# A 2-D spectral filter and a bilinear GLU on one core: down products gathered at five places of a chunk pair, and layer-norm operations one at each place

## The chip, the core and the metric

The kernel runs on one core of a Trainium2 chip. The metric is device time in microseconds for one execution. The kernel before takes 677.42 us, the median of three runs (677.13 to 677.56).

## The reference, cut to what matters

```
def _A_ref(x, w_r, w_i):
    X = rfft2(x) ; X = X * (w_r + 1j * w_i)
    return irfft2(X, s=(S, D))
def _B_ref(x, w_gate, w_up, w_down):
    g = x @ w_gate ; u = x @ w_up
    return (g * u) @ w_down
x = A_x                                   # S = 2048 tokens, D = 640, F = 1728
h  = x + _A_ref(_layernorm(x), A_w_r, A_w_i)
h2 = h + _B_ref(_layernorm(h), B_w_gate, B_w_up, B_w_down)
```

Everything is float32. The kernel splits each matmul operand into a high and a low part and multiplies high by high, high by low and low by high, so one product of 128 rows is three matmuls.

## The kernel before

Stages one and two (to about 190 us) are the spectral filter. Stage three is the bilinear GLU and takes the rest. Its 2048 tokens are two blocks of 1024, and its hidden width of 1728 is cut into chunks of 128; twelve whole chunks are taken as six pairs (`p` = 0 to 5), and a chunk pair is one step. The last columns are a step of their own (`p` = 6), which comes first in each block. Nothing reorders the work: every engine executes its instructions in the order in which this program writes them, and waits on counters of the other engines.

**Gate and up products.** `strassen()` (L1069) computes gate and up of one chunk with seven products on TensorE, six or nine matmuls of 512 columns each. Their sums live in PSUM banks from `single()`, four of them in rotation, of which a chunk takes three: `oa`, `ob` and `oc`. In traces these matmuls write `e`. ScalarE copies and VectorE additions and multiplications take the sums out: the copies `h0` (L1099), `c22` (L1109) and `h1` (L1116), and the VectorE lines L1119, L1122, L1123, L1129 and L1144. L1144 is the last reading of `oa`; it multiplies what the seventh product left there. In an odd chunk VectorE works out the seven left operands of the down products as well (L1131, L1134, L1155, and L1063 for the low parts, into the tile `ht`).

**Places.** After product n of a chunk the program calls `at(n)` (L1073), n from 1 to 7. Down products of the step before, layer-norm operations and preparations of weights (`side`) are hung there. So `at(1)` of a chunk stands between its first and its second product, and `at(7)` between its last product and the first of the next chunk.

**Down products.** A step's hidden activations meet the down weights one step later, beside the next pair's gate and up products. `down_products()` (L1025) does this with the seven-product algorithm, for two quarters of the tokens (`a` and `b`) in one call: fourteen products of three matmuls of 320 columns each. A step with such a pair before it (ten of the fourteen steps: `p` = 1 to 5 in both blocks) makes two calls, so 28 products. Each writes a PSUM bank from `lane()`, four banks, in traces `d`; a VectorE addition (L1044) then takes the whole bank into the residual rows `x`. A call uses a bank again and again, first clearing it or accumulating on what is there, so each product but the first in a bank waits for the addition before it in that bank. The order within a call is p1a p5a p1b p5b p6a p3a p6b p3b p7a p2a p7b p2b p4a p4b; p1, p6, p7 and p4 share one bank for `a` and one for `b`, p5, p3 and p2 the others. L1050 cuts a call into five pieces of 3, 3, 3, 2 and 3 products. L1303 and L1304 hang the ten pieces of a step at places 1 to 7 of the even chunk and 2 to 4 of the odd one.

**Layer norm of the second block.** While block 0 runs, the 32 small operations for the layer norm of block 1 (mostly `bn_stats` and `bn_aggr` on VectorE, L176 to L180) wait in a queue `fill`, and `at()` pops them from there. What is left is popped ahead of chunk 6.

Of the kernel before, what the change touches and what calls it, by code (L numbers as in the profile page):

```python
# [78 lines left out]
def tile_spectral_glu(ctx: ExitStack, tc: tile.TileContext, x, wre, wim, wgu, wlast, wdown, wdlast,  # L79
# [26 lines left out]
    def single():  # L106
        return bank("e", 4)
# [4 lines left out]
    def wk(shape, name):  # L112
        return work.tile(shape, F32, tag="wk", name=name)
# [4 lines left out]
    def mmx(o, l, r, start, stop):  # L118
        nc.tensor.matmul(o, l, r, start=start, stop=stop, skip_group_check=True)  # L119
# [3 lines left out]
    def pop(n=1):  # L123
        for _ in range(n):
            if fill:
                fill.popleft()()
# [87 lines left out]
    def front(ts, k):  # L214
        n = len(ts)
        r = small.tile([P, n], F32, tag="r", name="r")
        junk = [fold[:, o:o + D] for o in (NR * 1026, NR * 1026 + D)]
        m2, ve, fs = moments(ts, junk * 2 if k < n else None, k=k)
        for i, t in enumerate(ts):
            SC[t] = r[:, i:i + 1], m2[:, i:i + 1]  # L220
        return fs, inverse_root(ve, r, n)
# [10 lines left out]
    def even(t):  # L232
        f, j = folded(t)
        fs = [(0.47, lambda: nc.vector.scalar_tensor_tensor(view(f, 0, [[321, 2], [1, 161]]),
                                                     view(XP[t], 0, [[320, 2], [1, 161]]), SC[t][1],
                                                     view(XP[t], 640, [[-320, 2], [-1, 161]]),
                                                     op0=OP.subtract, op1=OP.add))]
        fs.append((0.14, lambda: tt(j[:, 0:64], f[:, 128:192], f[:, 449:513], op=OP.add)))
        fs.append((0.4, lambda: tt(view(j, 64, [[1, 2], [2, 160]]), view(f, 161, [[-161, 2], [1, 160]]),
                                   view(f, 482, [[-161, 2], [1, 160]]), op=OP.subtract)))  # L240
        return fs
# [58 lines left out]
    for ts, when, aside, root in GROUPS:  # L300
        k = len(when)
        fs, cs = front(ts, k)
# [15 lines left out]
    for t in range(NT):  # L318
        if t == 1:
            nc.gpsimd.dma_start(frall, frem)  # L320
        if t >= 1:
            fs = even(t)
# [422 lines left out]
    def scale_shift(ts, junk, total=None):  # L745
        n = len(ts)
        r = small.tile([P, n], F32, tag="r", name="r")
        b = small.tile([P, n], F32, tag="b", name="b")
        m2, ve, fs = moments(ts, junk, total)
        cs = inverse_root(ve, r, n)  # L750
        cs.append(lambda: nc.vector.scalar_tensor_tensor(b, m2, -0.5, r, op0=OP.mult, op1=OP.mult))
        for i, t in enumerate(ts):
            SC[t] = r[:, i:i + 1], b[:, i:i + 1]
        return fs, cs
# [108 lines left out]
    for ts in (range(3), range(3, 6), range(6, 8)):  # L863
        n, t0 = len(ts), ts[-1] + 1
        fs, cs = scale_shift(ts, [scrap] * n, total[:, ts[0]:t0])
# [120 lines left out]
    def operand(sb, k):  # L986
        return xt[:, sb, k, 0], xt[:, sb, k, 1]
# [71 lines left out]
    def hi_of(src, a):  # L1059
        act(hop[:, a, 0], src, AF.Copy)  # L1060

    def lo_of(src, a, engine=nc.vector):
        engine.tensor_tensor(hop[:, a, 1], src, f32(hop[:, a, 0]), op=OP.subtract)  # L1063
# [5 lines left out]
    def strassen(c, blk, ahead, downs, side):  # L1069
        wa, ws = W[c]  # L1070
        p, odd = divmod(c, 2)

        def at(n):  # L1073
            if downs.get(n):
                for f in downs[n]:
                    f()
                if c:
                    pop(2 if c in (2, 4) else 1)
            for f in side.get(n, ()):
                f()  # L1080

        b11, b21, b22 = ([operand(sb, k + i) for i in range(2)] for sb, k in ((0, 0), (0, 2), (1, 2)))
        t1, t2 = ([(TJ["12"][:, 0, m, k], TJ["12"][:, 1, m, k]) for k in range(2)] for m in range(2))
        t4 = [operand(1, k) for k in range(2)]
        b5 = [operand(sb, 4) for sb in range(2)]

        def product(o, first, w, a, ms, extra=()):
            terms = [(w, a + P * i, m) for i, m in enumerate(ms)] + list(extra)
            n = len(terms)
            for i, (w, a, m) in enumerate(terms):  # L1090
                whi, wlo = w[:, 0, a:a + P], w[:, 1, a:a + P]
                mmx(o, whi, m[0], first and i == 0, False)
                mmx(o, whi, m[1], False, False)
                mmx(o, wlo, m[0], False, i == n - 1)

        oa = single()
        product(oa, True, wa, 384, b11)
        h0 = wk([P, 512], "h0")
        act(h0, oa, AF.Copy)  # L1099
        for f in side.get(0, ()):  # L1100
            f()
        if ahead and c:
            ahead[0]()
            ahead[1]()
        at(1)
        ob = single()
        product(ob, True, ws, 256, t1, [(wa, 896, b5[1])])
        c22 = wk([P, 512], "c22")
        act(c22, ob, AF.Copy)  # L1109
        if not c:  # L1110
            ahead[0]()
            ahead[1]()
        at(2)
        product(oa, False, ws, 0, t2)
        h1 = wk([P, 512], "h1")
        act(h1, oa, AF.Copy)  # L1116
        at(3)
        product(ob, False, ws, 896, b22, [(ws, 512, b5[1])])
        tt(ob, ob, h1, op=OP.add)  # L1119
        at(4)  # L1120
        product(oa, False, ws, 640, [(t3[k][:, 0], t3[k][:, 1]) for k in range(2)])
        tt(c22, oa, c22, op=OP.add)  # L1122
        tt(ob if odd else h1, ob, c22, op=OP.mult)  # L1123
        if odd:
            hi_of(ob, 2 if p < 5 else 4)
        at(5)
        oc = single()
        product(oc, True, wa, 0, b21, [(wa, 256, b5[0])])
        tt(h0, oc, h0, op=OP.add)  # L1129
        if odd and p < 5:  # L1130
            tt(oc, ob, HELD["a21"], op=OP.add)  # L1131
            hi_of(oc, 3)
            lo_of(ob, 2)
            tt(ob, ob, HELD["s3"], op=OP.subtract)  # L1134
            hi_of(ob, 4)
            lo_of(oc, 3)
        elif odd:
            lo_of(ob, 4)
        if ahead and not odd:
            ahead[2]()  # L1140
            ahead[3]()
        at(6)
        product(oa, False, wa, 640, t4, [(wa, 896, b5[0])])
        tt(oa if c == 11 else h0, oa, h0, op=OP.mult)  # L1144
        if not odd:
            HELD["a11"], HELD["a21"] = h0, h1
            if p < 5:
                nc.gpsimd.tensor_tensor(c22, h0, h1, op=OP.subtract)
                HELD["s3"] = c22
        at(7)  # L1150
        if odd and p < 5:
            hi_of(h0, 1)
            lo_of(ob, 4)
            act(oc, h0, AF.Copy)
            tt(ob, h0, ob, op=OP.subtract)  # L1155
            hi_of(ob, 6)
            lo_of(oc, 1)
            lo_of(ob, 6)
        elif odd:
            hi_of(oa, 5)  # L1160
            lo_of(oa, 5)
# [5 lines left out]
    for n, (blk, p) in enumerate(steps):  # L1167
        if p == 6:
# [121 lines left out]
            if blk == 0:  # L1290
                fs, cs = scale_shift(range(8, 16), None)
# [5 lines left out]
        slots = [{}, {}]  # L1297
        if prev[1] == 6:
            fs = [[lambda j=j, prev=prev: down(*prev, j)] for j in range(8)]
            slots = [dict(zip(range(4, 8), fs[0:3] + [fs[3] + fs[4]])), dict(zip((2, 3, 4), fs[5:]))]  # L1300
        else:
            fs = down_products(*prev, (0, 1)) + down_products(*prev, (2, 3))
            slots[0] = dict(zip(range(1, 8), fs))  # L1303
            slots[1] = dict(zip((2, 3, 4), fs[7:]))  # L1304
        for ci in range(2):
            c = 2 * p + ci
            side = {n: [] for n in range(8)}
# [217 lines left out]
```

## Time and profile before

| | us |
|---|---|
| time, median of 3 | 677.42 |
| span of the profiled execution, first to last instruction | 675.8 |
| TensorE busy with matmuls | 663.8 |
| VectorE busy | 470.6 |
| GpSimd busy | 400.9 |
| ScalarE busy | 322.7 |

The time of the profiled execution itself isn't listed apart from the three runs; the median stands 1.6 us above the span. A row of the timeline gives start, duration, engine, line, operation, what it writes and reads, its shape and how many like it were merged. Matmuls are pipelined: a row's duration reaches past the start of the next row, so the rate of TensorE is read from one row's start to the next one's.

### The profile page before, as it was taken

Reading aid. Unit: us, or ns where it says so; the run is one execution under the profiler, and the core shown is the slowest. Engines: PE = TensorE matmul, PEld = TensorE weight load, DVE = VectorE, ACT = ScalarE, POOL = GpSimd, SP = SyncE. Lnnn points to the kernel's source line nnn. Section 1 sums busy time; section 2 is a strip of 40 time slices with the busy share of each in tenths; the row PEclk is TensorE's granted clock in tenths of the full one; section 3 lists DMA queues with packets and bytes.
Section 4 is the critical chain, followed back from the end, with each engine's and each line's share of the span. In section 5 each row is a group of like instructions: output and inputs, shape, how many; then the busy total and the mean of one; then the engine's idle time right before and its main releaser. Section 6 shows DMA issues by size and latency. Waiting matters only on the chain.

```text
span 675.8 us, 10232 instructions
## 1 busy us (share of the span) xinstructions
PE 663.8 (98%) x3695; PEld 587.9 (87%) x3695; DVE 470.6 (70%) x967; ACT 322.7 (48%) x622; POOL 400.9 (59%) x377
## 2 busy tenths in 40 slices
PE   7999999999999999999999999999999999999997
PEld 6998888887888888888888889888888888888887
DVE  6968887787866868585857657754757575756654
ACT  6977675485524344362626236534434252524220
POOL 3103334641198887878787544189687878787610
PEclk9999999999999999999999999999999999999999
DMA  9537964602212101143242458211012121212004
GB/s 321 220 101 247 266 225 153 178 22 78 79 40 78 40 37 42 40 108 69 86 90 79 97 109 281 78 41 59 21 39 79 40 78 40 79 39 80 1 0 156
DMA packets 46648, 66.11 MB, mean 98 GB/s; under 512 B 23826, under 2 KB 26318, under 8 KB 46470
## 3 DMA queue, kind: packets, MB, share of 16 engines
q1 hardware_dynamic: 45942, 62.90, 29.7%
q0 software_dynamic: 288, 2.16, 0.8%
q8 instruction: 29, 0.48, 0.3%
q10 hardware_dynamic: 368, 0.39, 0.2%
q14 instruction: 21, 0.17, 0.1%
HBM read 54.61 MB, written 10.84 MB: 97 GB/s over the span
## 4 chain that ended last, share of the span: by engine, by line
PE 89%; DMA 4%; DVE 3%; ACT 2%; issue 1%; SPq 0%; DVEq 0%; ACTq 0%
PE e L119 49%; PE d L119 26%; PE eo L119 4%; PE y L119 2%; PE im L252 2%; PE re L119 1%; PE u L454 1%; PE im L119 1%; PE im L506 1%; DMA bits<-in_mm_dram 1%; DMA wts<-in_wim_dram 1%; DMA sfar<-s1r 1%; DMA x<-in_x_dram 1%; PE ir L506 1%; ACT s L278 0%
## 5 line engine op out<-in xcount | busy, mean ns | idle before, releaser
L119 PE MATMUL e<-xt,wst 128*128 128x512 f32 x864 | 213.2, 391 | 0.0
L119 PEld LDWEIGHTS e<-xt,wst 128*128 128x128 f32 x864 | 159.8, 188 | 30.6
L1044 DVE TENSOR_TENSOR x<-d,x 128x320 f32<-128x320 f32 x280 | 123.4, 483 | 51.6 <-PE d L119 47.5
L119 PE MATMUL d<-wd,ht 128*128 128x320 f32 x832 | 143.6, 308 | 0.0
L119 PEld LDWEIGHTS d<-wd,ht 128*128 128x128 f32 x832 | 131.1, 188 | 7.6
L958 POOL TENSOR_TENSOR wst<-raw,wst 128x1024 fp32r<-128x1024 f32 x23 | 55.4, 2409 | 67.2 <-ACT wst L957 40.2
L119 PE MATMUL e<-t,wst 128*128 128x512 f32 x360 | 94.3, 392 | 0.0
L119 PEld LDWEIGHTS e<-t,wst 128*128 128x128 f32 x360 | 66.3, 188 | 12.6
L119 PE MATMUL d<-wt,ht 128*128 128x320 f32 x360 | 69.5, 310 | 0.0
L974 POOL TENSOR_TENSOR wst<-raw,wst 128x896 fp32r<-128x896 f32 (+1 forms) x46 | 65.1, 1436 | 0.2 <-ACT wst L969 0.2
L119 PEld LDWEIGHTS d<-wt,ht 128*128 128x128 f32 x360 | 57.3, 188 | 2.3
L1060 ACT ACTIVATE ht<-e 128x512 fp32r<-128x512 f32 x44 | 26.4, 599 | 51.5 <-DVE e L1123 25.9
L1099 ACT ACTIVATE h<-e 128x512 f32<-128x512 f32 x24 | 14.3, 595 | 67.3 <-PE e L119 67.3
L1019 DVE TENSOR_TENSOR x<-d,x 128x320 f32<-128x320 f32 x62 | 27.5, 485 | 23.5 <-PE d L119 23.5
L655 ACT ACTIVATE wd<-draw 128x320 fp32r<-128x320 f32 (+1 forms) x30 | 15.7, 558 | 57.5 <-POOL draw L665 54.3
L969 ACT ACTIVATE wst<-raw 128x896 fp32r<-128x896 f32 (+1 forms) x48 | 30.2, 677 | 26.5 <-POOL raw L963 25.7
L119 PE MATMUL e<-xt,wdir 128*128 128x512 f32 x180 | 42.0, 392 | 0.4 <-DVE w L207 0.2
L119 PEld LDWEIGHTS e<-xt,wdir 128*128 128x128 f32 x180 | 33.4, 188 | 8.1 <-ACT xt L780 0.7
L1119 DVE TENSOR_TENSOR e<-e,h 128x512 f32<-128x512 f32 x24 | 16.8, 699 | 30.8 <-PE e L119 17.7
L1063 DVE TENSOR_TENSOR ht<-e,ht 128x512 fp32r<-128x512 f32 x54 | 36.9, 685 | 1.6 <-ACT ht L1060 1.3
L634 POOL TENSOR_TENSOR wd<-draw,wd 128x640 fp32r<-128x640 f32 x8 | 12.4, 1576 | 40.5 <-ACT wd L633 40.5
L535 POOL CAST qr<-bits 1x128 fp32r<-1x128 f32 x15 | 12.1, 808 | 39.8 <-DVE qr L539 39.8
(234 smaller groups left out, 1199.3 us busy)
## 6 DMA issues: line engine op xcount, KB each, us to landing
raw<-in_wgu_dram SPq DMA_DIRECT2D x24, 640.0 KB
draw<-in_wdown_dram SPq DMA_DIRECT2D x24, 320.0 KB
wts<-in_wre_dram SPq DMA_DIRECT2D x16, 322.0 KB
x<-in_x_dram SPq DMA_DIRECT2D x15, 320.5 KB
out_dram<-x SPq DMA_DIRECT2D x15, 320.0 KB
bits<-in_mm_dram SPq DMA_DIRECT2D x16, 256.0 KB
wts<-in_wim_dram SPq DMA_DIRECT2D x9, 322.0 KB
zfar<-zr SPq DMA_DIRECT2D x32, 80.0 KB
```

Of the source, the lines that this page charges most:

```text
L119: nc.tensor.matmul(o, l, r, start=start, stop=stop, skip_group_check=True)
L252: nc.tensor.matmul(o, l, c, start=n == 0, stop=n == len(ls) - 1)
L655: act(o[:, 0, a:a + n], src, AF.Copy)
L958: ptt(wa[:, 1], stage[:, 0:1024], f32(wa[:, 0]), op=OP.subtract)
L969: act(ws[:, 0, o:o + b - a], stage[:, a:b], AF.Copy)
L974: ptt(ws[:, 1, o:o + b - a], stage[:, a:b], f32(ws[:, 0, o:o + b - a]), op=OP.subtract)
L1019: tt(xv, ps[b][:, 0:320], xv, op=OP.add)
L1044: tt(xv, o, xv, op=OP.add)
L1060: act(hop[:, a, 0], src, AF.Copy)
L1063: engine.tensor_tensor(hop[:, a, 1], src, f32(hop[:, a, 0]), op=OP.subtract)
L1099: act(h0, oa, AF.Copy)
L1119: tt(ob, ob, h1, op=OP.add)
```

## The change

The diff touches two places. In the ten steps whose predecessor is a pair, the ten pieces of the down products are joined two by two into runs of 6, 5, 6, 6 and 5 products, which hang at places 2, 4 and 6 of the even chunk and 2 and 4 of the odd one. And `at()` pops one layer-norm operation at each of the seven places of every chunk but chunk 0, whether down products hang there or not; before, it popped where down products hung, two in chunks 2 and 4 and one elsewhere.

```diff
         def at(n):
-            if downs.get(n):
-                for f in downs[n]:
-                    f()
-                if c:
-                    pop(2 if c in (2, 4) else 1)
+            for f in downs.get(n, ()):
+                f()
+            if c:
+                pop()
             for f in side.get(n, ()):
                 f()
...
             fs = down_products(*prev, (0, 1)) + down_products(*prev, (2, 3))
-            slots[0] = dict(zip(range(1, 8), fs))
-            slots[1] = dict(zip((2, 3, 4), fs[7:]))
+            runs = [a + b for a, b in zip(fs[0::2], fs[1::2])]
+            slots = [dict(zip((2, 4, 6), runs)), dict(zip((2, 4), runs[3:]))]
```

**TensorE at the start of an even chunk** (chunk 6 of block 1; a number marks one tile, and a wait names the engine whose counter is waited for). Before, with the first product (`e_5258`), place 1 and the start of the second product (`e_5289`):

```order
L119 MATMUL e_5258<-xt_1164,wst_5129 128x512 x3
L119 MATMUL d_5274<-wd_5015,ht_1736 128x320 [waits Activation_49]
L119 MATMUL d_5274<-wd_5015,ht_1736 128x320
L119 MATMUL d_5274<-wd_5015,ht_1736 128x320 [waits Pool_49]
L119 MATMUL d_5279<-wd_5015,ht_1736 128x320 [waits Activation_49]
L119 MATMUL d_5279<-wd_5015,ht_1736 128x320
L119 MATMUL d_5279<-wd_5015,ht_1736 128x320 [waits DVE_49]
L119 MATMUL d_5284<-wd_5015,ht_1736 128x320 x3
L119 MATMUL e_5289<-t12_3965,wst_5129 128x512 [waits DVE_49]
```

The same place in the change, where the second product writes `e_5274`:

```order
L119 MATMUL e_5258<-xt_1164,wst_5116 128x512 x3
L119 MATMUL e_5274<-t12_3965,wst_5116 128x512 [waits DVE_49,Activation_49]
L119 MATMUL e_5274<-t12_3965,wst_5116 128x512
L119 MATMUL e_5274<-t12_3965,wst_5116 128x512 [waits Pool_49]
L119 MATMUL e_5274<-t12_3965,wst_5116 128x512 x3
L119 MATMUL e_5274<-xt_1164,wst_5116 128x512 x3
L119 MATMUL d_5286<-wd_5003,ht_1736 128x320 x3
L119 MATMUL d_5291<-wd_5003,ht_1736 128x320 [waits Activation_49]
```

The three down products have gone from between the first and the second product to behind the second. The second product's first matmul waits for VectorE in both; in both programs the count waited for is that of the odd chunk's L1144, whose bank this second sum takes over.

**TensorE in the odd chunk at places 3 and 4** (chunk 7 of block 1). Before, with place 3, the fourth gate and up product (`e_5455`) and place 4:

```order
L119 MATMUL d_5398<-wd_5015,ht_1736 128x320 x3
L119 MATMUL d_5403<-wt_5016,ht_1736 128x320 x3
L119 MATMUL e_5455<-xt_1164,wst_5267 128x512 x9
L119 MATMUL d_5423<-wd_5015,ht_1736 128x320 x3
L119 MATMUL d_5393<-wt_5016,ht_1736 128x320 x3
L119 MATMUL d_5403<-wt_5016,ht_1736 128x320 x3
L119 MATMUL e_5439<-ht_1736,wst_5267 128x512 x3
```

The same in the change, with the fourth product (`e_5442`) and the run of five behind it:

```order
L119 MATMUL e_5442<-xt_1164,wst_5267 128x512 x9
L119 MATMUL d_5398<-wd_5003,ht_1736 128x320 x3
L119 MATMUL d_5403<-wt_5004,ht_1736 128x320 x3
L119 MATMUL d_5454<-wd_5003,ht_1736 128x320 x3
L119 MATMUL d_5393<-wt_5004,ht_1736 128x320 x3
L119 MATMUL d_5403<-wt_5004,ht_1736 128x320 x3
L119 MATMUL e_5426<-ht_1736,wst_5267 128x512 x3
```

The two products of bank `d_5403` (p7b, then p4b) had nine matmuls of 512 columns and two other products between them; now two other products alone stand between.

**VectorE at the end of chunk 1 of block 0.** Before:

```order
L1129 TENSOR_TENSOR h_2140<-e,h_2140 128x512
L1131 TENSOR_TENSOR e<-e,h_2002 128x512
L1063 TENSOR_TENSOR ht<-e,ht 128x512
L1134 TENSOR_TENSOR e<-e,c_1987 128x512
L1063 TENSOR_TENSOR ht<-e,ht 128x512
L1144 TENSOR_TENSOR h_2140<-e,h_2140 128x512
L1063 TENSOR_TENSOR ht<-e,ht 128x512
L1155 TENSOR_TENSOR e<-h_2140,e 128x512
```

In the change (every line number behind the diff's first hunk is smaller by one):

```order
L1128 TENSOR_TENSOR h_2140<-e,h_2140 128x512
L1130 TENSOR_TENSOR e<-e,h_2002 128x512
L1063 TENSOR_TENSOR ht<-e,ht 128x512
L1133 TENSOR_TENSOR e<-e,c_1987 128x512
L1063 TENSOR_TENSOR ht<-e,ht 128x512
L176 BN_STATS st<-x_78 128x6
L1143 TENSOR_TENSOR h_2140<-e,h_2140 128x512
L180 BN_AGGR mv<-st 128x2
L1063 TENSOR_TENSOR ht<-e,ht 128x512
L1154 TENSOR_TENSOR e<-h_2140,e 128x512
```

Layer-norm operations, popped at places 6 and 7, now stand among these operations. In chunk 3 of block 0 there are two `bn_stats` instead of one and a `bn_aggr`; in every later odd chunk the queue is empty by place 5.

## The prediction, as put on record

> **What bounds the kernel.** I read the page first, then busy time by windows, then the timelines of TensorE and VectorE around the places that the change touches.
>
> ```profile
> span 675.8 us, 10232 instructions
> ...
> PE 663.8 (98%) x3695; PEld 587.9 (87%) x3695; DVE 470.6 (70%) x967; ACT 322.7 (48%) x622; POOL 400.9 (59%) x377
> ...
> PE 89%; DMA 4%; DVE 3%; ACT 2%; issue 1%; SPq 0%; DVEq 0%; ACTq 0%
> ```
>
> ```profile
> 5.00:10.00 5.00, 2.96 (x27) 2.77 (x26) 4.72 (x19) 3.11 (x10) 2.76 (x5) 1.00 1.03 393
> 221.00:406.00 185.00, 185.00 (x968) 163.01 (x967) 129.95 (x264) 78.08 (x130) 137.51 (x118) 1.00 0.29 74
> 475.00:660.00 185.00, 185.00 (x962) 162.57 (x961) 116.83 (x228) 70.02 (x118) 132.86 (x115) 1.00 0.12 43
> ```
>
> The last two rows are the ten steps with the seven-product down products, five in each block: TensorE (the first busy column) is busy for 185.00 of 185.00 us. The chain that ended last is 89% TensorE. But busy matmuls overlap, so I check the rate from start to start:
>
> ```profile
> 536.99 0.60 PE L119 MATMUL d<-wd,ht 128*128 128x320 f32 x3
> 537.43 0.60 PE L119 MATMUL d<-wt,ht 128*128 128x320 f32 x3
> 537.87 2.23 PE L119 MATMUL e<-xt,wst 128*128 128x512 f32 x9
> 539.93 0.60 PE L119 MATMUL d<-wd,ht 128*128 128x320 f32 x3
> 540.37 1.04 PE L119 MATMUL d<-wt,ht 128*128 128x320 f32 x6
> 541.25 0.86 PE L119 MATMUL e<-ht,wst 128*128 128x512 f32 x3
> 541.94 0.85 PE L119 MATMUL e<-t,wst 128*128 128x512 f32 x3
> 542.63 5.60 PE L119 MATMUL e<-xt,wst 128*128 128x512 f32 x24
> 548.07 1.48 PE L119 MATMUL d<-wd,ht 128*128 128x320 f32 x9
> 549.39 1.55 PE L119 MATMUL e<-t,wst 128*128 128x512 f32 x6
> ...
> 551.91 0.68 PE L119 MATMUL d<-wt,ht 128*128 128x320 f32 x3
> ```
>
> Nine matmuls of 512 take 537.87 to 539.93, 0.229 us each; nine of 320 take 548.07 to 549.39, 0.147 each, so a down product of three is 0.44. The rows follow each other at these rates over every boundary: changing from `d` to `e` and back costs nothing. A step has 108 matmuls of 512 and 84 of 320: 24.7 + 12.3 = 37.0 us. The only irregular row is the last, 0.68 long where a row of three takes 0.60. There are six such rows in these steps, the first and the last of them:
>
> ```profile
> 258.63 0.68 PE L119 MATMUL d<-wt,ht 128*128 128x320 f32 x3
> 626.11 0.68 PE L119 MATMUL d<-wt,ht 128*128 128x320 f32 x3
> ```
>
> From 551.91 to 626.11 are two steps, 37.10 us each: the work itself. **So the change can gain six times 0.08 us, 0.5 us in all.** Everything else that it can do is to open waits in a TensorE that has none, and with no idle time in it no wait can be made up later. The question is which waits the pieces of down products cover now.
>
> **First part: place 1 of the even chunk is emptied.** Here is VectorE over the same stretch:
>
> ```profile
> 537.63 0.93 DVE L1044 TENSOR_TENSOR x<-d,x 128x320 f32<-128x320 f32 x2 [1.22 <-PE d L119]
> 540.20 0.70 DVE L1119 TENSOR_TENSOR e<-e,h 128x512 f32<-128x512 f32 x1 [1.64 <-ACT wst L969]
> 540.81 1.28 DVE L1044 TENSOR_TENSOR x<-d,x 128x320 f32<-128x320 f32 x3
> ...
> 544.87 0.69 DVE L1129 TENSOR_TENSOR h<-e,h 128x512 f32<-128x512 f32 x1 [0.61 <-PE e L119]
> 545.67 0.70 DVE L1131 TENSOR_TENSOR e<-e,h 128x512 f32<-128x512 f32 x1
> 546.27 0.68 DVE L1063 TENSOR_TENSOR ht<-e,ht 128x512 fp32r<-128x512 f32 x1
> 546.87 0.69 DVE L1134 TENSOR_TENSOR e<-e,c 128x512 f32<-128x512 f32 x1
> 547.47 0.68 DVE L1063 TENSOR_TENSOR ht<-e,ht 128x512 fp32r<-128x512 f32 x1
> 548.07 0.68 DVE L1144 TENSOR_TENSOR h<-e,h 128x512 f32<-128x512 f32 x1
> ...
> 551.28 1.28 DVE L1044 TENSOR_TENSOR x<-d,x 128x320 f32<-128x320 f32 x3
> ```
>
> The odd chunk's sixth product ends about 544.67, and from there VectorE runs five operations at about 0.6 us each ahead of L1144. L1144 therefore starts at 548.07, just where the even chunk's first product ends (first row of nine `d`), though the seventh product that it reads was over a product of six earlier. The even chunk's second product takes L1144's bank and waits for it. Before, nine `d` matmuls stood between, and it started at 549.39. In the change it is due at 548.07 and L1144 ends at 548.75. This wait is not in the trace of before; the nearest restart after a VectorE operation is the 0.68 row:
>
> ```profile
> 551.28 0.48 DVE L1044 TENSOR_TENSOR x<-d,x 128x320 f32<-128x320 f32 x1
> 551.88 0.44 PEld L119 LDWEIGHTS d<-wt,ht 128*128 128x128 f32 x3
> ```
>
> The addition ends at 551.76, the weights' load starts at 551.88, the matmul at 551.91: 0.15 after the addition, and 0.08 more is lost behind the first matmul. For the second product I take 0.15 alone, since the 0.229 of a matmul of 512 leaves room for the next load. The wait is 548.75 + 0.15 - 548.07 = **0.83 us**. Bounds: 0.68 if TensorE starts at L1144's end, 0.91 if the 0.08 is lost too. The structure is the same in all ten steps, and L1144's duration hardly varies:
>
> ```profile
> L1144 DVE TENSOR_TENSOR h<-e,h x22: 677/691/694, 196.9 to 641.1; 128x512 f32<-128x512 f32 x22
> ```
>
> Ten times 0.83 is 8.3 us (6.8 to 9.1). Nothing ahead of L1144 moves: VectorE was idle for 0.61 before L1129, so the longer run at the odd chunk's place 4 does not reach it.
>
> The Trainium skill ("TensorE: Matmul & The Clock Gate", section on what happens when you issue a matmul) says that TensorE pulls weight loads ahead of matmuls in flight. If that held past a wait, the lost 0.08 would not exist, and the run of five below would cost 0.15 each, 0.8 us less in all; but the row at 551.88 shows the load behind the wait, and the row decides.
>
> **Second part: runs of five and six.** A product reuses its bank four products later almost everywhere. With VectorE idle an addition starts 0.64 after its product does (536.99, 537.63) and takes 0.48, and additions follow each other every 0.40 (three in 1.28), quicker than the 0.44 of a product, so VectorE doesn't fall behind inside a run. The bank is free 0.64 + 0.48 + 0.15 = 1.27 after a product's start; four products are 1.76. Even where L1119 or L1129 comes first, the run's first addition starts at 0.88 (539.93, 540.81) and frees its bank at 1.51. No wait there. The run at place 2 of the even chunk starts at 548.90 + 2.06 = 550.96; its first addition at 551.60, after VectorE's backlog (551.28), frees the bank at 552.23, and the fifth product is due at 552.72. So the six 0.08 waits go: -0.5 us.
>
> One reuse is closer: in the last run, p2a p7b p2b p4a p4b at place 4 of the odd chunk, p4b takes p7b's bank three products later. L1119 stands ahead, so p7b's addition goes from 0.88 + 0.40 = 1.28 to 1.76, and p4b can start at 1.91 where it is due at 4 x 0.44 = 1.76: 0.15, and 0.08 behind the first matmul, 0.23 us. Bounds: 0, if VectorE keeps up as in an idle start (1.27 + 0.44 = 1.71), and 0.63, if one more operation of 0.40 stands ahead. Ten times: 2.3 us (0 to 6.3).
>
> The other gate and up products that come earlier by an emptied place (the fourth of both chunks, the sixth of the even one) wait for ScalarE copies or a free bank, with at least a run of five and a product between.
>
> **Third part: layer-norm operations at every place.** Their number is the same, and where VectorE waits for TensorE they are free. They cost where VectorE is late, at places 6 and 7 of an odd chunk: one `bn_stats` stands right ahead of L1144 in chunks 1 and 3 of block 0.
>
> ```profile
> 259.20 0.48 DVE L176 BATCH_NORM_STATS2 st<-x 128x6 f32<-128x320 f32 x1
> 259.60 0.19 DVE L180 BATCH_NORM_AGGREGATE mv<-st 128x2 f32<-128x12 f32 x1
> ```
>
> It occupies 0.40 (259.20 to 259.60). Two steps start their second product 0.40 later: 0.8 us (0 if hidden, 1.6 if both operations counted). What stands behind L1144 at places 7 and 1, up to 0.5, delays the first addition of the run at place 2 to 552.18; the bank is free at 552.81, the fifth product due at 553.12: hidden. Popping fewer in chunks 2 and 4 saves nothing, as no wait there is theirs.
>
> **The sum.** 8.3 + 2.3 + 0.8 - 0.5 = 10.9 us on the span: 675.8 + 10.9 = 686.7. The median stands 1.6 above the span (the profiled execution's own time is not given apart), so **688.3 us**, 1.6% slower. Bounds by all terms: 6.8 - 0.5 = 6.3 gives 683.7; 9.1 + 6.3 + 1.6 = 17.0 gives 694.4.
>
> **The rivals.**
> 1. *The run of five waits for nothing.* If L1119 lets the additions through in time, only the waits at the second product stay: 8.3 + 0.8 - 0.5 = 8.6, 686.0 us. For it: the margin is 0.15. Against: the row at 540.81 puts the additions behind L1119. 15%.
> 2. *VectorE is later than its rows.* If the run of five pays 0.63 and the second product 0.91, the time is 691 to 694.4. For it: five additions instead of three in a row. Against: 0.40 is less than 0.44. 10%.
> 3. *The clock falls.* TensorE now pauses ten times. If each pause halved the clock for the nine matmuls behind it (2.06 us), that is 20.6 more: 709 us. The Trainium skill (the same page, "A second HAM failure mode: psum-queue depth-cycling") describes short pauses between matmul groups that make the clock swing. Against it: between 5 and 10 us TensorE was busy for 2.96 of 5.00 and the granted clock was 1.00. 2%.
> 4. *Not slower.* VectorE runs its chain faster once no `d` banks are written beside it. The wait is gone if the five operations ahead of L1144 and L1144 itself end 0.83 sooner, about 0.46 each instead of 0.6; additions quicker by as much would clear the run of five too, and 0.5 us is gained: 676.9 us. Against it: in the row from 542.63 TensorE writes only `e` for 5.4 us, and VectorE takes 0.6 per operation beside it already. 5%, nearly all of it within 0.2%.
>
> That the change does not do what it says I give nothing: the order shows five runs, and the 32 layer-norm operations end at place 4 of chunk 5, before chunk 6 needs them.
>
> **How the numbers follow.** The forecast itself has 68%, from about 686.5 to 690.5. The range of 684.5 to 692.0 takes in the first rival and the lower part of the second, and leaves out the third, the fourth and the far ends of the bounds. Faster or slower by 0.2% (1.35 us) is about what a measurement of this kernel can tell from no change. Faster 1%, same 4%, slower 95%.
>
> **What would show it.** In the profile of the change TensorE should stand idle at the start of ten second products (`e<-t,wst`), released by VectorE's L1143 (L1144 before), 0.8 us each and 1.2 us at the steps behind chunks 1 and 3; ten rows of three `d` at the odd chunk's place 4 should be late by about 0.2, released by L1044; no late row at the even chunk's place 2; the granted clock 1.00. A step should be about 38.1 us long instead of 37.10. I am wrong if L1143 ends before the first product does, if the second product starts without waiting, or if the steps lengthen with no wait at these two places.

## The result, and the profile after

| | before | changed |
|---|---|---|
| time, median of 4 runs each, us | 677.39 (677.13 to 677.56) | 687.42 (687.22 to 687.51) |
| ratio, 95% interval | | 1.0143 (1.0129 to 1.0156) |
| span of the profiled execution, us | 675.8 | 685.7 |

The changed kernel is 1.4% slower, 10.0 us. The page of the changed kernel:

```profile
span 685.7 us, 10245 instructions
...
PE 667.5 (97%) x3695; PEld 588.3 (86%) x3695; DVE 474.2 (69%) x967; ACT 321.4 (47%) x622; POOL 401.1 (58%) x377
...
PE 87%; DVE 9%; ACT 2%; issue 1%; DMA 1%; DVEq 0%; ACTq 0%
```

VectorE has gone from 3% of the chain that ended last to 9%. Its busy time has hardly changed (470.6 to 474.2 us): it isn't slower, it is now waited for. Busy time by windows over the ten steps, with the columns of before (TensorE first, granted clock third from the end):

```profile
221.00:406.00 185.00, 181.97 (x942) 158.84 (x941) 128.47 (x255) 74.30 (x124) 133.21 (x116) 1.00 0.26 68
478.00:662.00 184.00, 180.69 (x935) 157.53 (x933) 115.28 (x224) 69.52 (x118) 132.92 (x116) 1.00 0.13 46
```

TensorE now stands still for 3 us in each block, at a clock of 1.00. The view of waits names the engine and line waited for, then us in total, how often, and the longest; the first row is of the matmuls, the second of the loads of weights:

```profile
PE e L119 <- DVE h L1143: 6.3, 9, 1.1
```

```profile
PEld d L119 <- DVE x L1044: 1.6, 10, 0.2
```

These are the two waits foretold, at the second product and in the run of five. The first row has nine of the ten waits (the view puts the one behind chunk 1 of block 0 down to another instruction) and counts from the end of the matmul before, which reaches past the next start. So the length of a wait is read from starts. TensorE in the step of chunks 5 and 6 of block 1, the one that the prediction shows of before:

```profile
547.41 1.21 PE L119 MATMUL d<-wt,ht 128*128 128x320 f32 x6
548.46 0.86 PE L119 MATMUL e<-ht,wst 128*128 128x512 f32 x3
...
549.85 5.61 PE L119 MATMUL e<-xt,wst 128*128 128x512 f32 x24
556.12 1.61 PE L119 MATMUL e<-t,wst 128*128 128x512 f32 x6 [0.66 <-DVE h L1143]
557.57 0.84 PE L119 MATMUL e<-xt,wst 128*128 128x512 f32 x3
558.25 1.92 PE L119 MATMUL d<-wd,ht 128*128 128x320 f32 x12
```

VectorE's row beside the gap:

```profile
555.30 0.68 DVE L1143 TENSOR_TENSOR h<-e,h 128x512 f32<-128x512 f32 x1
```

The 24 matmuls take 5.44 us as before, so the second product is due at 555.29. L1143 starts just then, ends at 555.98, and the product starts at 556.12: 0.83 late. Its six matmuls take 1.45 (556.12 to 557.57) where six at the rate of the 24 take 6 x 5.44 / 24 = 1.36: some 0.08 more is lost behind the first one. At the run of five, six matmuls take 1.05 (547.41 to 548.46) instead of 0.88. At the even chunk's place 2 the twelve `d` matmuls merge into one row, and none is late.

Behind chunk 3 of block 0, where a `bn_stats` stands ahead of L1143, TensorE and then VectorE show:

```profile
250.31 5.61 PE L119 MATMUL e<-xt,wst 128*128 128x512 f32 x24
256.98 1.63 PE L119 MATMUL e<-t,wst 128*128 128x512 f32 x6 [1.05 <-DVE h L1143]
```

```profile
255.76 0.48 DVE L179 BATCH_NORM_STATS2 st<-x 128x6 f32<-128x320 f32 x1
256.16 0.67 DVE L1143 TENSOR_TENSOR h<-e,h 128x512 f32<-128x512 f32 x1
```

Due at 250.31 + 5.44 = 255.75, started at 256.98: 1.23 late, 0.40 more than elsewhere.

### The profile page after: what moved, and what is told of

Same layout as the page of the kernel before. It is cut to its first block, busy times and chain, and to the rows that moved or that the text cites. A ratio compares the mean times of both kernels' runs of the same rounds, so it can differ in the third digit from the quotient of the medians.

```text
span 685.7 us, 10245 instructions
## 1 busy us (share of the span) xinstructions
PE 667.5 (97%) x3695; PEld 588.3 (86%) x3695; DVE 474.2 (69%) x967; ACT 321.4 (47%) x622; POOL 401.1 (58%) x377
## 4 chain that ended last, share of the span: by engine, by line
PE 87%; DVE 9%; ACT 2%; issue 1%; DMA 1%; DVEq 0%; ACTq 0%
PE e L119 44%; PE d L119 26%; PE eo L119 4%; PE u L454 2%; PE re L119 2%; PE y L119 2%; PE im L119 2%; PE im L506 2%; DVE ht L1063 2%; PE im L252 2%; DVE h L1128 1%; DVE e L1130 1%; PE ir L506 1%; DVE e L1133 1%; DVE h L1143 1%
## 5 line engine op out<-in xcount | busy, mean ns | idle before, releaser
L119 PE MATMUL e<-xt,wst 128*128 128x512 f32 x864 | 210.7, 390 | 0.0
L119 PEld LDWEIGHTS e<-xt,wst 128*128 128x128 f32 x864 | 161.5, 188 | 33.0
L119 PEld LDWEIGHTS d<-wd,ht 128*128 128x128 f32 x832 | 129.3, 188 | 4.4
L1098 ACT ACTIVATE h<-e 128x512 f32<-128x512 f32 x24 | 14.3, 595 | 61.5 <-PE e L119 61.5
L1115 ACT ACTIVATE h<-e 128x512 f32<-128x512 f32 x24 | 14.3, 597 | 61.2 <-PE e L119 61.2
```

## The experiments

Ratios are against the kernel before, timed beside it; its median was 677.42 to 677.74. Diffs are against the changed kernel unless said otherwise.

### The two waits, taken away one at a time

**e4_p7b_first.** The close reuse of one bank goes, nothing else: p7b and p2a change places, so that p4b comes four products behind p7b.

```diff
             fs = down_products(*prev, (0, 1)) + down_products(*prev, (2, 3))
+            fs[8] = fs[8][::-1]
             runs = [a + b for a, b in zip(fs[0::2], fs[1::2])]
```

> The change, with p7b ahead of p2a in the second call's fourth piece, so that p4b in the run of five finds p7b's bank used four products earlier instead of three. Theory: the ten waits of about 0.165 in that run go, everything else stays: 685.8 us. Rival (the lost time in that run is not the bank's reuse but the five additions as such): no change, 687.4 us.

Measured: 685.81 us, 1.0124 (1.0108 to 1.0139). TensorE in the run of five:

```profile
584.17 1.04 PE L119 MATMUL d<-wt,ht 128*128 128x320 f32 x6
585.05 0.85 PE L119 MATMUL e<-ht,wst 128*128 128x512 f32 x3
```

The last six matmuls take 0.88 again (584.17 to 585.05). One swap of two products is worth 1.6 us, so this wait was the reuse, at about 0.16 a step.

**e3_first_run_split.** The first run of six is split again: three products go back to place 1.

```diff
-            slots = [dict(zip((2, 4, 6), runs)), dict(zip((2, 4), runs[3:]))]
+            slots = [{1: fs[0], 2: fs[1], 4: runs[1], 6: runs[2]}, dict(zip((2, 4), runs[3:]))]
```

> The change, but its first run of six is cut in two: three products go back to place 1 of the even chunk and three stay at place 2; the other four runs and the layer-norm operations stay as in the change. Theory: the ten waits at the second product (8 x 0.90 + 2 x 1.29 = 9.8 us) go, the late rows of 0.08 at place 2 come back in most steps, the run of five keeps its ten waits of about 0.165, and four changes between d and e fewer than before gain some 0.02 each per step: 677.4 + 1.65 - 0.84 = 678.2 us. Rival (runs of five and six are slow because VectorE can't empty four banks fast enough): four of five long runs are left, so at least 684 us.

Measured: 679.49 us, 1.0029 (1.0017 to 1.004).

```profile
544.30 5.60 PE L119 MATMUL e<-xt,wst 128*128 128x512 f32 x24
549.74 1.48 PE L119 MATMUL d<-wd,ht 128*128 128x320 f32 x9
551.05 1.55 PE L119 MATMUL e<-t,wst 128*128 128x512 f32 x6
```

Nine `d` matmuls stand between again, and the second product starts on time (549.74 + 1.31 = 551.05) in all ten steps. That is 7.9 of the 10.0 us. It is 1.3 more than expected: place 2 of chunks 2 and 4 of block 0 now has a wait of its own (0.43 and 0.81, with 0.08 behind each), which e1, below, shows by itself.

**e5_one_op_behind** and **e6_two_ops_behind.** The places stay as in the change; VectorE's backlog ahead of L1143 is made shorter instead. e5 moves the low part of `oc` (`lo_of(oc, 3)`) alone behind L1143; e6 moves the subtraction from `ob` and `ob`'s high part, a ScalarE operation, as well:

```diff
             lo_of(ob, 2)
-            tt(ob, ob, HELD["s3"], op=OP.subtract)
-            hi_of(ob, 4)
-            lo_of(oc, 3)
...
         tt(oa if c == 11 else h0, oa, h0, op=OP.mult)
+        if odd and p < 5:
+            tt(ob, ob, HELD["s3"], op=OP.subtract)
+            hi_of(ob, 4)
+            lo_of(oc, 3)
```

> The change, with one of VectorE's operations that stand ahead of the odd chunk's last multiplication (L1143 in the change) moved behind it: the low part of operand 3, about 0.6 us. Matmuls and places are those of the change. Theory (the second product waits for the end of that multiplication, which VectorE's backlog delays): each of the ten waits shrinks by 0.6, from 0.90 to 0.30 and from 1.29 to about 0.7, 6 us in all: 681.4 us. Rival (the wait is for VectorE's whole backlog or for the emptied place as such): 687.4 us, or the same time lost in the run behind it.

> As the run before, with two operations moved behind that multiplication (the difference for operand 4 and the low part of operand 3), 1.2 us. Theory: the multiplication is over before the second product is due, so the ten waits (9.8 us) are gone; the run of six then starts 0.9 earlier and meets the backlog again, as in the runs with products at place 1: about 0.08 in most steps and 0.43 and 0.81 in the two steps behind chunks 1 and 3 of block 0, 1.7 us in all: 679.4 us. Rival (an emptied place 1 costs whatever VectorE's order): 685 us or more.

Measured: 682.36 us, 1.0069 (1.0057 to 1.0082), and 682.06 us, 1.0065 (1.0052 to 1.0077). TensorE in e5:

```profile
546.39 5.61 PE L119 MATMUL e<-xt,wst 128*128 128x512 f32 x24
552.07 1.62 PE L119 MATMUL e<-t,wst 128*128 128x512 f32 x6
```

VectorE's row of the multiplication, which is L1142 here:

```profile
551.24 0.68 DVE L1142 TENSOR_TENSOR h<-e,h 128x512 f32<-128x512 f32 x1
```

The wait is 552.07 - 546.39 - 5.44 = 0.24, against 0.83: one operation of 0.6 less on VectorE takes 0.6 from it, and the product again starts 0.15 after the multiplication's end (551.92), so the wait is the backlog. The time is 1.0 us above what was expected. Two small new waits at place 2 in block 0 (0.12 and 0.18, with 0.08 behind each) are 0.5 of it, and the kernel before was 0.3 slower beside this run than beside the change. In e6 the wait at the second product is gone, but not the time; TensorE, then VectorE:

```profile
553.75 1.92 PE L119 MATMUL d<-wd,ht 128*128 128x320 f32 x12
555.76 0.68 PE L119 MATMUL d<-wt,ht 128*128 128x320 f32 x3
```

```profile
553.71 1.51 DVE L1063 TENSOR_TENSOR ht<-e,ht 128x512 fp32r<-128x512 f32 x2
555.14 2.07 DVE L1044 TENSOR_TENSOR x<-d,x 128x320 f32<-128x320 f32 x5
```

Twelve `d` matmuls take 1.76, so the row at 555.76 is due at 555.51: 0.25 late and 0.08 behind it. What was put behind L1143 now stands ahead of the additions at 555.14, which free the banks of the run of six. The wait moved to the next place. I had expected it there at 0.08 in eight of the ten steps; it is 0.20 to 0.27 and 0.08 behind, and e6 is 2.7 us above what was expected.

### The two halves of the change, alone

**e1_pops_only.** The new `at()` with the ten places of before.

```diff
-            runs = [a + b for a, b in zip(fs[0::2], fs[1::2])]
-            slots = [dict(zip((2, 4, 6), runs)), dict(zip((2, 4), runs[3:]))]
+            slots[0] = dict(zip(range(1, 8), fs))
+            slots[1] = dict(zip((2, 3, 4), fs[7:]))
```

> The layer-norm half of the change alone: down products at the ten places of before, one layer-norm operation at each place. Theory (two waits, at the second product of the even chunk and in the run of five): place 1 of the even chunk covers L1144's end with 0.49 us to spare, and a bn_stats takes 0.40 of it in two steps, so nothing opens: 677.4 us, within 0.4 of before. Rival (operations at every place hold VectorE up and are a cost of their own): 680 us or more, with waits in chunks 1 to 5 of block 0.

Measured: 678.80 us, 1.0018 (1.0009 to 1.0026), a miss: it costs about 1.2 us. TensorE at place 2 of chunk 4:

```profile
258.25 0.60 PE L119 MATMUL d<-wd,ht 128*128 128x320 f32 x3
259.49 0.68 PE L119 MATMUL d<-wt,ht 128*128 128x320 f32 x3 [0.64 <-DVE x L1044]
```

The second row is due at 258.69 and 0.80 late; chunk 2 has the same at 0.43. The layer-norm operations popped at places 6, 7 and 1 stand in VectorE's backlog ahead of the additions, and p6a waits for one of these. In the change the wait at the second product comes first and covers it.

**e2_places_only.** Five places with the `at()` of before, which pops only where down products hang.

```diff
-            for f in downs.get(n, ()):
-                f()
-            if c:
-                pop()
+            if downs.get(n):
+                for f in downs[n]:
+                    f()
+                if c:
+                    pop(2 if c in (2, 4) else 1)
```

> The five places alone, layer-norm operations popped as before. Theory: eight waits of 0.90 at the second product stay, the two of 1.29 behind chunks 1 and 3 shrink to 0.90, so 0.8 us less than the change: 686.6 us. Rival (operations at every place are a cost of their own): 684 us or less.

Measured: 689.69 us, 1.0179 (1.0165 to 1.0193), another miss, 3 us up. The ten waits at the second product are there, all of 0.82 now: the two of 1.2 behind chunks 1 and 3 have shrunk as expected. But with fewer places only 19 of the 32 layer-norm operations are popped before chunk 6; 13 stand in one piece ahead of it. VectorE's first and last rows of these, and the additions behind:

```profile
296.66 0.48 DVE L179 BATCH_NORM_STATS2 st<-x 128x6 f32<-128x320 f32 x1
...
299.64 0.17 DVE L751 SCALAR_TENSOR_TENSOR b<-m,r 128x8 f32<-128x8 f32 x1
299.73 2.67 DVE L1044 TENSOR_TENSOR x<-d,x 128x320 f32<-128x320 f32 x6
```

TensorE beside them:

```profile
296.40 1.92 PE L119 MATMUL d<-wd,ht 128*128 128x320 f32 x12
300.36 0.68 PE L119 MATMUL d<-wt,ht 128*128 128x320 f32 x3 [2.04 <-DVE x L1044]
```

It waits for these additions from 298.16 (twelve `d` matmuls after 296.40) to 300.36, and then busy time by windows shows something that no other profile of these kernels has:

```profile
297.00:300.50 3.50, 1.46 (x10) 1.23 (x10) 3.02 (x14) 1.94 (x4) 0.22 (x1) 1.00 0.00 0
...
302.00:303.00 1.00, 1.00 (x4) 0.71 (x4) 1.00 (x2) 0.30 (x1) 0.92 (x2) 0.50 0.00 0
304.00:305.00 1.00, 1.00 (x4) 0.81 (x3) 0.19 (x1) 1.00 (x3) 0.92 (x2) 0.50 0.45 68
306.00:320.00 14.00, 14.00 (x75) 12.38 (x74) 8.61 (x17) 3.25 (x6) 11.13 (x12) 1.00 0.53 104
```

The granted clock is 0.50 from about 302 to 305, after the pause is over, and 1.00 again from 306. Not every execution has this: of e2's four, two took 690.66 (the one profiled) and 690.39 us at mean granted clocks of 0.997 and 0.998, the other two 688.85 and 689.00 at 0.999 and 1.000. So the layer-norm half of the change isn't decoration: without it the five places cost some 1.5 us more where the clock holds and 3.1 where it falls.

### Is there a version without waits?

**e9_before_two_behind.** The lines of e6's diff applied to the kernel before, to ask if VectorE's order there has slack.

> The kernel before, ten places and its own popping, with only the two operations moved behind the multiplication. Theory: place 1 covered that wait already, so nothing changes: within 0.3 us of before. It separates the five places from the new order in the run before this one. Rival (the new order of VectorE is a gain by itself): 676.5 or less.

Measured: 679.92 us, 1.0031 (1.002 to 1.0043), a miss. The waits of its weights' loads:

```profile
PEld d L119 <- DVE ht L1063: 1.5, 10, 0.2
```

The down products at place 1 now wait ten times for the low part that was moved. So the order of before has no slack for these operations: moved behind the multiplication, they make place 1 wait in the kernel before and place 2 in the change.

**e7_two_behind_swap_spread.** e6 and e4 together, with the layer-norm operations spread to places where VectorE waits for TensorE (beside the lines of those two diffs):

```diff
-            if c:
-                pop()
+            if c % 2:
+                pop({1: 2, 2: 1, 3: 1, 4: 1}.get(n, 0))
+            elif c:
+                pop({2: 2, 3: 1, 4: 2, 5: 1, 6: 2, 7: 1}.get(n, 0))
```

> All waits found so far taken away with the five places kept: two operations behind the multiplication, p7b ahead of p2a, and the layer-norm operations at places where VectorE is not late (odd chunks: two at place 1, one at 2, 3 and 4; even chunks: 2, 1, 2, 1, 2, 1 at places 2 to 7). Theory: what is left of the change is five changes between d and e fewer per step, about 0.02 each: 1.05 us less than before, and at most 0.08 per step at p6a: 676.0 to 676.9 us against 677.4 before, on this chip in the same proportion. Rival (fewer changes gain nothing): 677.4 or more.

Measured: 679.32 us, 1.0024 (1.0014 to 1.0034). A miss by e6's remaining wait, 0.20 to 0.27 and 0.08 in each of the ten steps, some 3.2 us.

**e8_split_swap_spread.** e3, e4 and e7's spreading; VectorE's own order stays as before. Beside the lines of e7's diff:

```diff
+            fs[8] = fs[8][::-1]
             runs = [a + b for a, b in zip(fs[0::2], fs[1::2])]
-            slots = [dict(zip((2, 4, 6), runs)), dict(zip((2, 4), runs[3:]))]
+            slots = [{1: fs[0], 2: fs[1], 4: runs[1], 6: runs[2]}, dict(zip((2, 4), runs[3:]))]
```

> Six places: three products at place 1 of the even chunk, three at place 2, and the change's other four runs, with p7b ahead of p2a and the layer-norm operations at places where VectorE is not late. VectorE's own order is that of before. Theory: no wait at the second product, none in the run of five, the late rows of 0.08 at place 2 as before, and four changes between d and e fewer per step at about 0.02: 0.8 us under before on the same chip. Rival (fewer changes gain nothing): the same as before or above.

Measured: 676.86 us, 0.9989 (0.998 to 0.9998), as expected. No wait in the ten steps but the six small late rows of before, and one more like them. With e3's 679.49 the spreading and the swap are worth 2.6 us.

**e10_five_other_places.** e7's spreading, and five places again, others than the change's: 1, 3 and 6 of the even chunk, 2 and 4 of the odd one.

```diff
-            runs = [a + b for a, b in zip(fs[0::2], fs[1::2])]
-            slots = [dict(zip((2, 4, 6), runs)), dict(zip((2, 4), runs[3:]))]
+            fs[3] = fs[3][::-1]
+            slots = [{1: fs[0], 3: fs[1] + fs[2], 6: fs[3] + fs[4]}, {2: fs[5] + fs[6], 4: fs[7] + fs[8] + fs[9]}]
```

> Five places as in the change, but others: three products at place 1 of the even chunk (the cover of before), six at place 3, five at place 6 with p7b first, and in the odd chunk six at place 2 and eight at place 4; layer-norm operations at places where VectorE is not late. Theory: no wait at all, since the run behind place 1 comes only after VectorE's backlog; five changes between d and e fewer per step (1.05 us) and the six late rows (0.5 us) gone: 1.5 us under before on the same chip. Rival (runs of five to eight are slow for TensorE or VectorE in themselves): 2 us or more above before, as in the change.

Measured: 679.45 us, 1.0025 (1.0016 to 1.0033), a miss:

```profile
540.84 1.27 PE L119 MATMUL d<-wt,ht 128*128 128x320 f32 x6
541.94 0.85 PE L119 MATMUL e<-ht,wst 128*128 128x512 f32 x3
```

1.10 where 0.88 is due: the eight products at place 4 end with p4b three behind p7b, the same close reuse in another run. I had swapped p7b and p2a in the first call alone, and in the odd chunk the second call's order stood as before. The profiled execution took 678.35; what made the median 1.1 us longer its trace doesn't show.

**e11_five_places_no_reuse.** The same places, with the odd chunk's runs in an order in which no bank comes back within a run in fewer than four products (place 4: p3b p7b p7a p2a p2b p4b p4a).

Against e10:

```diff
-            slots = [{1: fs[0], 3: fs[1] + fs[2], 6: fs[3] + fs[4]}, {2: fs[5] + fs[6], 4: fs[7] + fs[8] + fs[9]}]
+            two = sum(fs[5:], [])
+            slots = [{1: fs[0], 3: fs[1] + fs[2], 6: fs[3] + fs[4]},
+                     {2: two[0:7], 4: [two[i] for i in (7, 10, 8, 9, 11, 13, 12)]}]
```

> As the run with five other places, but the odd chunk's products stand in another order so that no bank is used again after fewer than four products: seven at place 2, and p3b p7b p7a p2a p2b p4b p4a at place 4. Theory (the loss of 0.2 per step there came from p4b three products behind p7b, however long the run): no late row in any of the ten steps, five changes between d and e fewer per step and no row of 0.08: about 1.5 us under before on the same chip. Rival (a run of seven or eight is late for itself): 1 to 2 us above before, as in that run.

Measured: 676.83 us, 0.9991 (0.9982 to 1.0), 0.6 us below before, at the edge of what the interval can tell, and not the 1.5 expected. Nine steps have no wait; in chunk 4 of block 0 (the next expectation calls it chunk 3) TensorE waits for 1.1 us behind an operation of eight elements on VectorE. That operation, and GpSimd's beside it:

```profile
266.92 2.15 DVE L182 TENSOR_SCALAR m<-mv 128x8 f32<-128x8 f32 x1
```

```profile
266.91 2.13 POOL L974 TENSOR_TENSOR wst<-raw,wst 128x896 fp32r<-128x896 f32 x1
```

Both start at 266.9 and end at 269.0 to 269.1. L182 takes at most 0.18 us in the kernel before.

**e12_doubling_on_scalar.** That operation on ScalarE, against e11:

```diff
-            fs.append(lambda: nc.vector.tensor_scalar(m2[:, 0:n], mv[:, :, 0], 2.0, None, op0=OP.mult))
+            if n == 8:
+                fs.append(lambda: act(m2[:, 0:n], mv[:, :, 0], AF.Identity, scale=2.0))
+            else:
+                fs.append(lambda: nc.vector.tensor_scalar(m2[:, 0:n], mv[:, :, 0], 2.0, None, op0=OP.mult))
```

> The five other places without the close bank reuse, and the doubling of eight means (L182, one small VectorE operation that took 2.15 us there and ended as GpSimd's operation beside it ended) on ScalarE, which stands idle there from about 265.1 to 271.8 us. Theory: VectorE lost 2.0 us because its small operation was shut out by GpSimd's, and that alone made TensorE wait 1.1 us in chunk 3 of block 0. Without it no step of stage three has a wait, all ten take 36.90 us, and the time is 0.6 + 1.1 = 1.7 us below before, about 675.7 (ratio 0.9975). Rival: VectorE was late there for other reasons, or its next small operation with operands in SBUF alone (L183, 0.15 us now) is shut out in its place; then the wait stays and the time is 676.8 as without this edit. Second rival: ScalarE's extra operation waits for VectorE's bn_aggr and holds up ScalarE's copies; then a wait on ScalarE shows, and the time is above 676.8.

Measured: 676.16 us, 0.9977 (0.9968 to 0.9986), span 673.9. ScalarE's row (the edit's lines move the numbers; L183 is the doubling) is

```profile
265.48 0.21 ACT L183 ACTIVATE m<-mv 128x8 f32<-128x8 f32 x1 [4.55 <-DVE mv L180]
```

and the view of waits is empty for matmuls and for loads from 190 us to 670; in the ten steps a single row, in chunk 5 of block 0, is still 0.1 late. It beats both kernels: five places, other than the change's, are better than ten once nothing waits for them. Whether they are better than e8's six isn't shown: the two intervals overlap, and e8 left the doubling on VectorE.

## Why the prediction was right

It said 688.3 us, 684.5 to 692.0, and the time was 687.42. To check its terms one needs a step without any wait, which e12 gives. From the first to the last of these rows are five steps of block 1, before, after and in e12:

```profile
468.49 5.60 PE L119 MATMUL e<-xt,wst 128*128 128x512 f32 x24
653.93 4.24 PE L119 MATMUL e<-xt,wst 128*128 128x512 f32 x18
```

```profile
473.88 5.60 PE L119 MATMUL e<-xt,wst 128*128 128x512 f32 x24
663.85 4.24 PE L119 MATMUL e<-xt,wst 128*128 128x512 f32 x18
```

```profile
467.53 5.60 PE L119 MATMUL e<-xt,wst 128*128 128x512 f32 x24
652.03 4.24 PE L119 MATMUL e<-xt,wst 128*128 128x512 f32 x18
```

They take 185.44, 189.97 and 184.50: a step is 37.09, 37.99 and 36.90.

| term, us in all | predicted | measured |
|---|---|---|
| second product, ten times | 8.3 | 9.0: 0.83 late as said, and 0.08 behind it |
| `bn_stats` ahead, two steps | 0.8 | 0.8 |
| run of five, ten times | 2.3 | 1.65 |
| late rows gone | -0.5 | -0.5 |
| fewer changes from `d` to `e` | 0 | about -1.3 |
| sum | 10.9 | about 9.7; the span grew by 9.9 |

That the sum is within 1.0 is in part luck: the second product cost 0.7 more than forecast, the run of five 0.65 less, and the last term had been left out.

- **Emptied place 1: right in place, cause and size.** e3 takes these waits away by putting `d` matmuls between, e5 shortens them by shortening the backlog. What failed is the sentence that 0.229 of a matmul of 512 leaves room for the next load: the 0.08 is lost there too, the upper bound of 0.91 that I had set. The rule on weight loads weighed there (the Trainium skill, "TensorE: Matmul & The Clock Gate", section on what happens when you issue a matmul), by which that 0.08 would not exist, doesn't reach past a wait in this trace either: the load of the second product stands at 556.09, behind L1143's end at 555.98.
- **The run of five: right mechanism, too large.** e4 shows that it is the reuse of p7b's bank. TensorE's load of weights and VectorE's additions in the change:

```profile
585.91 0.45 PEld L119 LDWEIGHTS d<-wt,ht 128*128 128x128 f32 x3 [0.16 <-DVE x L1044]
```

```profile
584.97 2.18 DVE L1044 TENSOR_TENSOR x<-d,x 128x320 f32<-128x320 f32 x5
```

  The additions start every 0.40 (the last, which waits for its own product, a little later), so the second ends at 584.97 + 0.40 + 0.48 = 585.85. That is 1.76 behind the start of the run at 584.09, just what the prediction has. The step of it that was mis-sized is the restart: the load follows at 585.91 and the matmul with it, 0.05 behind the addition and not the 0.15 that I had taken from another row; 0.10 instead of 0.08 goes behind the first matmul. The run loses 1.05 - 0.88 = 0.17 in place of 0.23.
- **"Changing from `d` to `e` and back costs nothing": wrong.** The prediction's own rows held it: nine `e` matmuls right behind `d` take 2.06, nine of the 24 in a row 9 x 5.44 / 24 = 2.04. A step of e12 has five such changes, one of before ten, and it is 0.19 shorter, of which the late rows are 0.06 (four in five steps, 0.08 each); the rest is 0.13 a step, about 0.025 a change. e8, with six changes, stands between: its steps without a late row take 36.96, those of before 37.04. The cost can be seen in the rows of single matmuls too: in block 1 of before, the first five matmuls of 512 behind `d` products stand 231, 236, 228, 233 and 231 ns apart (medians), and 227 from the sixth on, 24 ns in all. So gathering could gain more than the 0.5 us that I gave as its limit: e12 gained 1.4. Why the first five are slower stays open.
- **Layer norm: right, under a condition.** The prediction takes what stands behind L1144 at places 7 and 1 as hidden, with the late start of the run at place 2 in its sum. It is hidden only because of that late start: where the run starts on time (e1, e3), the same operations cost 1.2 us.
- **The rivals.** The run of five did wait, so the first is out. Of the second, the 0.91 at the second product came, the 0.63 in the run of five did not. VectorE's chain ran no faster without `d` beside it: L1143 starts at 555.30, as late against the first product as L1144 did. The clock stayed at 1.00 through ten pauses of 0.8 to 1.2 us, but the profile of e2 shows it fall behind one of about 2.2.

## What to carry to other kernels

Where the bounding engine has no idle time, look at each gap in its dependences for what covers it: the three down products at place 1 did no good by where they stood except that TensorE had something to do while VectorE caught up, and taking them away cost 0.9 us a step. Reordering such a backlog moves the wait to what needs the operations that were put last (e9), or to what now stands behind them (e6); leaving the cover where it is and gathering other pieces (e8, e12) gained. Check each gathered run for the distance at which a bank comes back: three products were too close and four were not, in both runs where it was tried. That holds where VectorE's additions start without a backlog: in e6 and e7 p6a waits for a bank used four products earlier.

## What the runs showed of the hardware

**A small VectorE operation can wait out a whole GpSimd operation.** All instances of L182 in a kernel, by duration in ns (least, median, most), before and in e11:

```profile
L182 DVE TENSOR_SCALAR m<-mv x5: 155/160/177, 6.3 to 263.0; 128x2 f32<-128x2 f32 x3, 128x1 f32<-128x1 f32 x1, 128x8 f32<-128x8 f32 x1
```

```profile
L182 DVE TENSOR_SCALAR m<-mv x5: 154/161/2148, 6.5 to 266.9; 128x2 f32<-128x2 f32 x3, 128x1 f32<-128x1 f32 x1, 128x8 f32<-128x8 f32 x1
```

In the changed kernel VectorE and GpSimd show the same on a smaller scale:

```profile
268.27 0.72 DVE L182 TENSOR_SCALAR m<-mv 128x8 f32<-128x8 f32 x1
```

```profile
266.55 2.41 POOL L656 TENSOR_TENSOR wd<-draw,wd 128x320 fp32r<-128x320 f32 x2
```

Where L182 took long it ended within 0.03 us of a GpSimd operation: 268.99 and 268.96 here, 269.07 and 269.04 in e11. Over all the profiles, L182 and L183 (the like operation behind it; L186 in e12) took longer than 0.3 us nineteen times, in eleven kernels, and each time ended 0.024 to 0.030 us after a GpSimd operation did. The Trainium skill ("SBUF — State Buffer", section on who interferes with whom) says that VectorE and GpSimd share one pair of ports as an exclusive lock, that a `tensor_scalar` may take it, and that whoever comes second blocks fully; the trace agrees. e12 shows that TensorE's wait ends with the operation moved to ScalarE, where it takes 0.21; that the lock is the reason is inferred from these coinciding ends.

**Half clock after a pause of some 2.2 us.** In the profile of e2 the granted clock fell to 0.50 about 1.5 us after TensorE had started again, for some 3 us. The pause was 300.36 - 298.16 = 2.20. The Trainium skill ("TensorE: Matmul & The Clock Gate", section "What's actually happening") has the clock fall after an idle window of about 3.4 us; here a shorter pause was enough, though a wait of 0.8 lay some four us ahead of it. Which length decides was not tried, and two of e2's four executions show no such loss in their mean clock.

**The restart after a wait is not one number.** TensorE's matmul started 0.14 us after VectorE's operation ended at the second product, and its load of weights about 0.05 after it in the run of five; behind the first matmul 0.08 and 0.10 more went. In the slower case the trace has a wait for a semaphore as an instruction of its own ahead of the load (556.02 to 556.07), as in the late row of before (551.80 to 551.85); in the run of five it has none.
